# Full-size transposes in a routed mixture of experts: padded gathered rows, a padded threshold, comparisons counted in pairs and a new order

## The chip, the cores and the metric

One core of one Trainium2 chip runs the whole program in one launch. The metric is the device time of an execution in microseconds (us); a kernel's time is the median of several executions. A profiled execution is a separate one and has its own time.

## What is computed

The program chains three stages: masked attention, a two-layer network with a squared ReLU, and a mixture of 8 experts with a greedy assignment of tokens. The change touches the third, whose reference is

```python
def _moe2_ref(x, w_gate, w1, w2):
    N, D = x.shape                      # 1536, 512
    E = w_gate.shape[1]                 # 8
    cap = N // E                        # 192
    flat = (x @ w_gate).flatten()
    order = np.argsort(-flat)
    assigned = -np.ones(N, dtype=np.int64)
    counts = np.zeros(E, dtype=np.int64)
    for idx in order:
        tok, e = (int(idx) // E, int(idx) % E)
        if assigned[tok] >= 0 or counts[e] >= cap:
            continue
        assigned[tok] = e
        counts[e] += 1
        if (assigned >= 0).all():
            break
    out = np.zeros((N, D), dtype=np.float32)
    for e in range(E):
        mask = assigned == e
        h = np.maximum(x[mask] @ w1[e], 0.0)      # w1[e] 512x1024
        out[mask] = h @ w2[e]                     # w2[e] 1024x512
    return out
```

Every expert ends with exactly 192 tokens, its cap.

## The kernel before, in words

Attention takes the first 260 us, the two-layer network runs to about 545 us, router and experts to the end. All matrix work goes through the one instruction queue of TensorE (PE). PSUM banks are named psS, psTP, psm, psO; ff and rf are the zones of SBUF that the third stage uses (rf for fp32r data and raw weights), f and r those of the first two.

**The router** finds the assignment in 8 phases. A phase ranks the remaining tokens by their best logit (rank): for each tile of 128 tokens VectorE (DVE, L1357), or ScalarE for some tiles (ACT, L1353 and L1355), makes a 0/1 tile G in bf16 that compares all values with those of the tile, and PE multiplies each G with the tiles' choices Bb (L1364), 12 matmuls for 12 tiles, later 9 and 6 for fewer tokens. There are four G buffers for DVE. The sums tell which expert fills first and at which value. That threshold is a minimum over tokens and partitions (rest): L1404 reduces to 128x8, L1409 transposes it on PE to 8x128, L1412 reduces that to a column xm of 8 rows, L1415 transposes the column, broadcast, back to all partitions, and L1417 goes on from there. The rest of a phase takes the full expert's tokens out and packs their numbers with the slot constants (L1477) into ix (L1487). The slot constants are four casts on GpSimd (POOL, L1088). The counts are bf16 and nearly everything else on PE is fp32. Short bf16 filler matmuls (L1094) are put on PE where the planner sees it idle.

**An expert** p, in the order in which experts fill, has 192 tokens. POOL gathers their rows with two indirect DMAs (L1676), 128 rows into g[0] and 64 rows into g[1], and then copies the expert's number (L1681), on which the loads of weight groups 1 to 3 wait; group 0 is loaded from the first copy. SyncE (SP) reads the number (L1671) and issues the loads of w1 and w2 (L1633, L1634), 512 KB each. xt_pe transposes the gathered rows, two calls of four transposes: 128x128 ones for the first 128 rows (L1694) and 64-row ones for the other 64 (L1696). The 192 columns of each half are evacuated by ACT and DVE (L1708, L1710; from expert 5 on L1701, L1703). The first layer is L1790 (experts 0 to 4, 128x192 outputs) or L1748 and L1749 (experts 5 to 7); its results go through ReLU by L1801 on ACT and L1804 on DVE (later L1757, L1760, L1762, L1765) and the second layer is L1861 to L1868, where L1868 handles 64 of the 192 rows. Weights are split into two parts by L1644 (ACT) and L1646 (DVE, for some of expert 6's on POOL). Results are scaled by L1924 to L1928 and scattered by L1915 (POOL).

**What sets the order.** Nothing is ordered by hand. A list planner (class Sched) gets every step as an operation with an engine, an assumed duration, the operations that it needs, a priority and the buffers that it takes and releases. Each engine takes the ready operation with the best priority; going between bf16 and fp32 work on PE has an assumed extra. The instructions are issued in the planned order, and semaphores follow the dependencies. The priorities are the numbers in three tables: EP (L1008, the early part of the router), RP (L1016, its phases) and FP (L1594, the experts).

A step in the planner's terms, here the count of one tile:

```python
c.append(S.add("PE", .0252 * n, lambda k=k: g_pe(k), [a, st["z"], st["Bb"], c[-1] if c else None], prio=RP["gp"], w=CW, half=1))
```

Of the kernel before, what the change touches and what calls it, by code (L numbers as in the profile page):

```python
# [7 lines left out]
F32 = mybir.dt.float32  # L8
R = mybir.dt.float32r
BF = mybir.dt.bfloat16  # L10
F16 = mybir.dt.float16
# [993 lines left out]
    return [ld[n] for n in range(12)], st, [i for f in range(16) for i in Wd[f]], []  # L1005


EP = {"fr": 1921.5, "lr": -1861, "row": -1588, "col": 174, "cp": 2028, "ca": -84.5, "gp": 1193}  # L1008
CP = (5, 2, 4, 2, 1, 0)
CA = (3, 0, 2, 4, 1, 4)  # L1010
EP_POOL = (3, 6, 8)
# [1 line left out]
HUGE = 1.5e38  # L1013
SQUEEZE = (2, 4)
ND = 4
RP = {"fr": 2216, "se": 1209, "oh": -1168.5, "G": 471, "A": -1078.5, "lr": -1735.5, "pf": -2953, "id": -1707, "gp": -701, "sq": 1077, "G1": -1034, "A1": 839, "ei": -1539.5, "up": -1158.5}  # L1016
ACT_TILES = {12: (10, 11), 9: (8,), 6: ()}
KEEP = 60
CW = .05
# [17 lines left out]
class Router:  # L1037
# [18 lines left out]

    def pools(self, tc, ctx):
        c = ctx.enter_context(tc.tile_pool(name="rcs2", bufs=1))
        for nm, shape, dt in (("alive", [12], F32), ("pad", [1], F32), ("zero", [128], BF), ("ones", [128], BF), ("tri", [128], BF), ("tok", [12], F16),
                              ("L1", [9, 8], F32), ("alive1", [9], F32), ("tok1", [9], F16),  # L1060
                              ("L2", [6, 8], F32), ("alive2", [6], F32), ("tok2", [6], F16)):
# [8 lines left out]
    def smalls(self, S, deps):  # L1070
        k, P = self.k, self.nc.gpsimd
        alive, tok = self.alive, self.tok

        def small():
            P.memset(alive, 1.0)
            P.memset(self.alive1, 1.0)
            P.memset(self.alive2, 1.0)
            P.memset(self.zero, 0.0)
            P.memset(self.ones, 1.0)
            P.tensor_copy(self.tri, k[:, 0:128])  # L1080
            P.tensor_copy(tok, k[:, 272:284])
        return [S.add("POOL", 1.5, small, deps, prio=MB + 60)]
# [260 lines left out]
    def rank(self, st, ph):  # L1343
        nc, S, n = self.nc, self.S, self.n
        V = nc.vector
        T = self.T
        W = 128 * n

        def g_dve(k, part):
            s = T["mx"][:, k:k + 1]  # L1350
            G, Gt = (self.mem(x, [W], BF) for x in (T["G", k], self.GT))
            if part == 1:
                nc.scalar.activation(Gt, T["lr"], AF.Relu, scale=-1.0, bias=s)  # L1353
            elif part == 2:
                nc.scalar.activation(G[:, 0:W], Gt, AF.Sign)  # L1355
            else:
                V.tensor_scalar(G[:, 0:W], T["lr"], s, None, op0=OP.is_lt)  # L1357

        def g_pe(k):
            Rv = T["R"][:, 0:8 * n].rearrange("p (i e) -> p i e", e=8)  # L1360
            G = self.mem(T["G", k], [W], BF)
            done.append(k)
            for i in range(n):
                nc.tensor.matmul(Rv[:, i], G[:, 128 * i:128 * i + 128], T["Bb"][:, k], start=False, stop=(len(done) == n and i == n - 1))  # L1364

        act = ACT_TILES.get(n, ())
        done = []
        gp = {"a": [], "d": []}
        gt = None
        for k in [*act, *(k for k in range(n) if k not in act)]:  # L1370
            w = "a" if k in act else "d"
            c = gp[w]
            m = 2 if k in act else 4
            war = c[-m] if len(c) >= m else None
            T["G", k] = (self.GA if m == 2 else self.G)[len(c) % m]
# [5 lines left out]
            c.append(S.add("PE", .0252 * n, lambda k=k: g_pe(k), [a, st["z"], st["Bb"], c[-1] if c else None], prio=RP["gp"], w=CW, half=1))  # L1381
        st["rank"] = st["lr"] = [c[-1] for c in gp.values() if c]
        st["unit"] = "B"


    def rest(self, st, ph):
# [8 lines left out]
        def dve(dur, fn, deps, p=RP["se"], rel=None):  # L1395
            return S.add("DVE", dur, fn, deps, prio=p, rel=rel)
# [194 lines left out]
        st["L"], st["alive"], st["tok"] = a, None, e1  # L1591


FP = {"s1": -1097, "ga": -1236, "xp": 853.5, "xe": -539.5, "m1": 866, "re": -510.5, "m2": 30.5, "ye": -493.5, "yt": 339, "yo": -2034, "sc": -2189.5, "sp": -163, "mr": 866}  # L1594
AP = 5
HP, XP = 0, 5
RSLACK, ESLACK = 0, 0.2
# [12 lines left out]
def experts(tc, nc, S, ps, mem, ident, router, x2d, w1, w2, out, L, cst, slot):  # L1610
# [6 lines left out]
    def unit(key, r):  # L1617
        return S.unit(T[key], r)
# [44 lines left out]
    def xr(p):  # L1663
        return "xT" if p < XP else "xR"

    def before(p):
        RT, ids, ei = next(phases)
        RTs[p] = RT

        def vl(i):  # L1670
            T["ev", p, i] = nc.sync.value_load(RT["ei"][0:1, i:i + 1], min_val=0, max_val=7)  # L1671

        def gather():
            g = xg(p)
            for h, n in ((0, 128), (1, 64)):
                nc.gpsimd.indirect_dma_start(out=g[h][0:n], out_offset=None, in_=x2d, in_offset=bass.IndirectOffsetOnAxis(ap=RT["ix"][0:n, h:h + 1], axis=0))  # L1676

        T["v", p, 0] = S.add("SP", .1, lambda: vl(0), [ei], prio=p)
        weights(p, 0, 0)
        T["ga", p] = ga = S.add("POOL", 2.7 if p else 3.8, gather, [ids], prio=FP["ga"], acq="xg")  # L1680
        e2 = S.add("POOL", .1, lambda: nc.gpsimd.tensor_copy(RT["ei"][:, 1:2], RT["ei"][:, 0:1]), [ga, ei], prio=-1)  # L1681
        gd = S.add("DMA", 1.2, None, [ga], prio=-1, lat=1.8)
        T["v", p, 1] = S.add("SP", .1, lambda: vl(1), [e2], prio=p)

        def tv(q):
            return ps(unit(("xt", p, q), "B"))[:, 0:384].rearrange("p (c s) -> p c s", c=2)

        def xt_pe(q):
            g = xg(p)
            for h in (0, 1) if q == 0 else (1, 0):  # L1690
                for c in range(2):
                    cc = 2 * q + c
                    if h == 0:
                        nc.tensor.transpose(tv(q)[:, c, 0:128], g[0][:, 128 * cc:128 * cc + 128], ident)  # L1694
                    else:
                        nc.tensor.transpose(tv(q)[:, c, 128:192], g[1][0:64, 128 * cc:128 * cc + 128], ident[0:64, 0:64])  # L1696

        def xt_hl(q, j):
            o = xT(p)[:, 2 * q:2 * q + 2]
            if j == 0:  # L1700
                nc.scalar.activation(o[:, :, 0], tv(q), AF.Copy)  # L1701
            else:
                nc.vector.tensor_tensor(o[:, :, 1], tv(q), o[:, :, 0].bitcast(F32), op=OP.subtract)  # L1703

        def xt_ev(q):
            o = xT(p)[:, 2 * q:2 * q + 2]
            if q == 0:
                nc.scalar.activation(o, tv(q), AF.Copy)  # L1708
            else:
                nc.vector.tensor_copy(o, tv(q))  # L1710

        xd, a = [], None
        for q in range(2):
            T["xt", p, q] = a = S.add("PE", .44, lambda q=q: xt_pe(q), [gd, a], prio=FP["xp"], acq=("B",) if q else ("B", xr(p)), rel=[("xg", ga)] if q else (), w=.6)
# [327 lines left out]
```

## Time and profile before

| | |
|---|---|
| median of 3 executions | 769.29 us (769.22 to 770.6) |
| the profiled execution | 773.7 us |
| its span | 771.9 us |
| mean granted clock of TensorE | 0.986 |
| PE busy | 751.4 us, 97% of the span |
| DVE busy | 562.4 us, 73% |
| ACT busy | 451.1 us, 58% |
| POOL busy | 399.7 us, 52% |
| DMA | 94.33 MB, mean 122 GB/s |

Busy shares are means over three stages with different limits. The stage of router and experts is read from the timeline and the waits of its own stretch. In the rows below a start is when the engine began an instruction or a run of equal ones, the second column is how long the row lasted, and PE rows overlap, since PE takes the next matmul while the last one runs out: what an instruction costs in a row of others is the distance between starts. "64*128" in a PE row is a tile of 64 rows of the array.

### The profile page before, as it was taken

How to read it: one execution, taken by the hardware profiler on the slowest of the kernel's cores; microseconds unless marked ns; L12 is line 12 of the kernel's file. 1: busy time of each engine (PE TensorE's matmuls, PEld its weight loads, DVE VectorE, ACT ScalarE, POOL GpSimd, SP SyncE). 2: the span in 40 equal slices, each digit the busy share in tenths (PEclk: the TensorE clock that was granted, in tenths of full speed). 3: DMA queues.
4: the chain of work that ended last, by engine and by line, in shares of the span. 5: the costliest groups of instructions: out<-in, count | busy, mean ns of one | idle time of the engine just before them, and what ended most of it. 6: DMA issues, size and time to landing. Idle time of an engine off the chain costs nothing.

```text
span 771.9 us, 13993 instructions
## 1 busy us (share of the span) xinstructions
PE 751.4 (97%) x4950; PEld 655.8 (85%) x4950; DVE 562.4 (73%) x1171; ACT 451.1 (58%) x900; POOL 399.7 (52%) x401
## 2 busy tenths in 40 slices
PE   8989999999999999999999999999999999999996
PEld 6768889879897899999999999999768888888885
DVE  5869989989899967831771484134897888888883
ACT  6969999989998855542343334224443543345772
POOL 2667778768788975752463365215921112222621
PEclk9999999999999999999999999999889999999998
DMA  6976586476640141410131110020136466478901
GB/s 157 244 165 144 115 175 150 102 159 143 157 103 2 56 164 64 153 57 1 55 113 51 53 58 1 0 82 28 56 114 235 154 229 212 152 259 312 349 26 37
DMA packets 87973, 94.33 MB, mean 122 GB/s; under 512 B 41920, under 2 KB 66880, under 8 KB 87904
## 3 DMA queue, kind: packets, MB, share of 16 engines
q1 hardware_dynamic: 85856, 87.16, 40.0%
q0 software_dynamic: 2048, 6.29, 2.6%
q8 instruction: 39, 0.64, 0.3%
q14 instruction: 30, 0.25, 0.1%
HBM read 63.55 MB, written 6.29 MB: 90 GB/s over the span
## 4 chain that ended last, share of the span: by engine, by line
PE 74%; DVE 8%; issue 5%; POOL 4%; ACT 4%; DMA 3%; SPq 1%; ACTq 0%; POOLq 0%; DVEq 0%
PE psS L829 11%; PE psTP L802 9%; PE psm L802 9%; PE psS L1790 6%; PE psS L578 4%; DVE p L626 3%; PE psTP L829 3%; PE psO L829 3%; PE psTP L614 2%; DVE f L594 2%; PE psS L1865 2%; PE psS L1861 2%; POOL f L606 2%; PE psS L1868 2%; PE psS L1862 2%
## 5 line engine op out<-in xcount | busy, mean ns | idle before, releaser
L606 POOL TENSOR_TENSOR f<-f 128x768 f32<-128x768 f32 x96 | 140.8, 1469 | 30.2 <-PE psTP L614 10.2
L815 POOL TENSOR_TENSOR r<-f,r 128x384 fp32r<-128x384 f32 x64 | 86.6, 1359 | 90.5 <-ACT r L813 77.9
L594 DVE TENSOR_REDUCE f<-psS 128x1 f32<-128x768 f32 x96 | 90.9, 948 | 7.6 <-PE psS L578 7.4
L829 PE MATMUL psS<-r 128*128 128x512 f32 x384 | 95.9, 395 | 0.0
L578 PE MATMUL psS<-r 128*128 128x384 f32 x384 | 88.4, 352 | 1.4 <-DMA r<-r 0.8
L597 ACT ACTIVATE f<-psS,f 128x768 f32<-128x768 f32 x96 | 87.1, 907 | 4.2 <-DVE f L603 1.4
L811 DVE TENSOR_TENSOR f<-f,psTP 128x384 f32<-128x384 f32 x32 | 17.7, 554 | 88.7 <-ACT f L809 88.4
L829 PEld LDWEIGHTS psS<-r 128*128 128x128 f32 x384 | 70.8, 188 | 13.1
L802 PE MATMUL psTP<-r 128*128 128x384 f32 x384 | 73.4, 338 | 0.7 <-POOL r L792 0.7
L802 PE MATMUL psm<-r 128*128 128x384 f32 x384 | 71.8, 334 | 0.0
L802 PEld LDWEIGHTS psTP<-r 128*128 128x128 f32 x384 | 67.9, 188 | 3.1 <-POOL r L792 1.0
L578 PEld LDWEIGHTS psS<-r 128*128 128x128 f32 x384 | 65.9, 190 | 5.3 <-ACT f L597 3.3
L802 PEld LDWEIGHTS psm<-r 128*128 128x128 f32 x384 | 67.1, 188 | 0.1
L1915 POOL DMA_INDIRECT out_dram<-ff,ix x16 | 17.9, 1116 | 83.8 <-DVE ff L1926 27.0
L1790 PE MATMUL psS<-ff,rf 128*128 128x192 f32 x320 | 61.0, 332 | 0.0
L626 DVE TENSOR_TENSOR p<-psTP,p 128x384 fp32r<-128x384 f32 x102 | 54.8, 546 | 4.9 <-ACT p L622 4.5
L813 ACT ACTIVATE r<-f 128x384 fp32r<-128x384 f32 x64 | 33.5, 523 | 39.3 <-DVE f L811 39.3
L1676 POOL DMA_INDIRECT ff<-x2d,ix x16 | 19.4, 1210 | 69.9 <-DVE ck L1549 17.7
L792 POOL TENSOR_TENSOR r<-f,r 128x1024 fp32r<-128x1024 f32 x16 | 40.4, 2526 | 28.4 <-ACT r L790 28.1
L1644 ACT ACTIVATE ff<-rf 128x1024 fp32r<-128x1024 f32 x32 | 33.8, 1055 | 34.8 <-PE psS L1863 25.2
L622 ACT ACTIVATE p<-psTP 128x384 fp32r<-128x384 f32 x102 | 49.3, 499 | 7.6 <-PE psTP L614 6.4
L1790 PEld LDWEIGHTS psS<-ff,rf 128*128 128x128 f32 x320 | 52.0, 190 | 1.9 <-DVE ff L1710 0.3
(400 smaller groups left out, 1860.9 us busy)
## 6 DMA issues: line engine op xcount, KB each, us to landing
rf<-in_moe_w_dram SPq DMA_DIRECT2D x64, 512.0 KB, 4.0
r<-r SPq DMA_DIRECT2D x90, 192.0 KB, 4.0
f<-in_moe_w_in_dram SPq DMA_DIRECT2D x16, 512.0 KB, 3.7
f<-in_moe_w_out_dram SPq DMA_DIRECT2D x16, 512.0 KB
r<-r SPq DMA_DIRECT2D x15, 384.0 KB
f<-in_q_dram SPq DMA_DIRECT2D x8, 384.0 KB
f<-in_k_dram SPq DMA_DIRECT2D x8, 384.0 KB
f<-in_v_dram SPq DMA_DIRECT2D x8, 384.0 KB, 3.8
```

The source lines that it names most:

```text
L578: nc.tensor.matmul(sbank(u)[:, hf, 0:384], T["q", (pr, h)][:, n, 128 * i:128 * i + 128], T["k", (pr, h)][:, n, 384 * hf:384 * hf + 384], s ...
L594: nc.vector.tensor_reduce(col(0, u), sbank(u)[:, :, 0:384], axis=AX.XY, op=OP.max, negate=True)
L597: nc.scalar.activation(P(u).rearrange("p (a b) -> p a b", a=2), sbank(u)[:, :, 0:384], AF.Exp, bias=col(0, u), accum_out=col(1, u))
L606: nc.gpsimd.tensor_tensor(Pn(u), P(u), col(3, u).to_broadcast([128, 768]), op=OP.mult)
L622: nc.scalar.activation(th, tp(u, g), AF.Copy)
L626: nc.vector.tensor_tensor(tl, tp(u, g), th.bitcast(F32), op=OP.subtract)
L792: nc.gpsimd.tensor_tensor(lo, F, hi.bitcast(F32), op=OP.subtract)
L802: nc.tensor.matmul(hbank(s, hf), w[:, c], y[:, x, sl], start=(c == 0 and i == 0), stop=(c == 3 and i == 2))
L815: nc.gpsimd.tensor_tensor(hl[:, sl], r, hh[:, sl].bitcast(F32), op=OP.subtract)
L829: nc.tensor.matmul(abank(i), a[:, t], w, start=(f == RUNS[r][1][0] and j == 0), stop=(f == RUNS[r][1][-1] and j == 2))
L1644: nc.scalar.activation(h(p, g, 0), w, AF.Copy)
L1790: nc.tensor.matmul(abank(n)[:, j], raw(p, g)[:, 0, 256 * c + 128 * j:256 * c + 128 * j + 128], xT(p)[:, c], start=(c == 0), stop=(c == 3))
```

## The change

1. The gathered rows are always transposed as 128x128: g[1] is read over all 128 rows. Its rows 64 to 127 are set to zero once by a new POOL operation (two memsets of 64x512, one for each of the two buffers), and the gather writes only rows 0 to 63. The evacuations read the first 192 of 256 columns. Both calls now take g[0] first.
2. The column xm is a lasting 128x1 tile, zeroed once; the transpose that spreads it (L1415) is 128x128 in place of 8 rows to 8 columns.
3. On DVE's tiles the counts are issued for two tiles together, as one operation of the planner, save the last two tiles (LONE). ACT's tiles are counted alone as before.
4. The three tables have other numbers, and so the planner finds another order for router and experts. Attention and the two-layer network keep theirs.

```diff
-EP = {"fr": 1921.5, "lr": -1861, ...
+EP = {"fr": 1831, "lr": -1863.5, ...
+LONE = 2
-RP = {"fr": 2216, "se": 1209, ...
+RP = {"fr": 2209, "se": 1249, ...
...
+            P.memset(self.xm, 0.0)
...
-        def g_pe(k):
+        def g_pe(ks):
             Rv = T["R"][:, 0:8 * n].rearrange("p (i e) -> p i e", e=8)
-            G = self.mem(T["G", k], [W], BF)
-            done.append(k)
-            for i in range(n):
-                nc.tensor.matmul(Rv[:, i], G[:, 128 * i:128 * i + 128], T["Bb"][:, k], start=False, stop=(len(done) == n and i == n - 1))
+            for k in ks:
+                G = self.mem(T["G", k], [W], BF)
+                done.append(k)
+                for i in range(n):
+                    nc.tensor.matmul(Rv[:, i], G[:, 128 * i:128 * i + 128], T["Bb"][:, k], start=False, stop=(len(done) == n and i == n - 1))
...
+            pend.append((k, a))
+            if len(pend) == 2 or ds.index(k) >= len(ds) - LONE:
+                c += [S.add("PE", .0252 * n * len(pend), lambda ks=[x[0] for x in pend]: g_pe(ks), [*(x[1] for x in pend), st["z"], st["Bb"], c[-1] if c else None], prio=RP["gp"], w=CW, half=1)] * len(pend)
+                pend.clear()
...
-        a = dve(.2, lambda: V.tensor_reduce(t("xm", [1])[0:8], T["xp"][0:8, 0:128], axis=AX.X, op=OP.min), [a])
+        a = dve(.2, lambda: V.tensor_reduce(self.xm[0:8], T["xp"][0:8, 0:128], axis=AX.X, op=OP.min), [a])
         def y_pe():
-            nc.tensor.transpose(T["xp"][:, 128:136], T["xm"][0:8].to_broadcast([8, 128]), self.ident[0:8, 0:8])
+            nc.tensor.transpose(T["xp"][:, 128:256], self.xm.to_broadcast([128, 128]), self.ident)
...
-FP = {"s1": -1097, "ga": -1236, ...
+FP = {"s1": -1161.5, "ga": -1309.5, ...
...
-            for h in (0, 1) if q == 0 else (1, 0):
+            for h in range(2):
                 for c in range(2):
                     cc = 2 * q + c
-                    if h == 0:
-                        nc.tensor.transpose(tv(q)[:, c, 0:128], g[0][:, 128 * cc:128 * cc + 128], ident)
-                    else:
-                        nc.tensor.transpose(tv(q)[:, c, 128:192], g[1][0:64, 128 * cc:128 * cc + 128], ident[0:64, 0:64])
+                    nc.tensor.transpose(tv(q)[:, c, 128 * h:128 * h + 128], g[h][:, 128 * cc:128 * cc + 128], ident)
...
+    def pad():
+        for u in UNITS_F["xg"]:
+            nc.gpsimd.memset(mem(u + 2, [512])[64:128], 0.0)
+    T["pad"] = S.add("POOL", 1.0, pad, L, prio=-3)
```

**PE, the transposes of expert 1's gathered rows** (L1694 and L1696 are L1705 after the change; behind them L1326, transposes of the router's next phase, is L1328). Before:

```order
L1865 MATMUL psS_5659<-ff_5223,rf_5214 128x512
L1868 MATMUL psS_5659<-ff_5224,rf_5214 64x512
L1694 MATMUL psTP_60<-ident,ff_5227 128x128 x2
L1696 MATMUL psTP_60<-ident,ff_5227 128x64 x2
L1696 MATMUL psTP_61<-ident,ff_5227 128x64 x2
L1694 MATMUL psTP_61<-ident,ff_5227 128x128 x2
L1326 MATMUL psO<-ident,mx 128x128 x4
```

After:

```order
L1874 MATMUL psS_5664<-ff_5225,rf_5216 128x512
L1877 MATMUL psS_5664<-ff_5226,rf_5216 64x512
L1705 MATMUL psTP_60<-ident,ff_5229 128x128 x4
L1705 MATMUL psTP_61<-ident,ff_5229 128x128 x4
L1328 MATMUL psO<-ident,mx 128x128 x4
```

The place is the same; the four 64-column outputs became 128-column ones.

**PE, counts and second layer in the phase of 9 tiles**, some 3 us further on. A count block is 9 pairs of LDWEIGHTS and MATMUL (L1364 before, L1367 after). Before, one block stood between the two halves of a group of the second layer (L1865, L1868):

```order
L1364 MATMUL psTP_61<-Bb,ff_5237 128x8
L1865 MATMUL psS_5659<-ff_5220,rf_5212 128x512
L1868 MATMUL psS_5659<-ff_5220,rf_5212 64x512
L1364 LDWEIGHTS ff_5238
L1364 MATMUL psTP_61<-Bb,ff_5238 128x8
```

After, the group stands together and the counts of two tiles follow it:

```order
L1799 MATMUL psS_5256<-ff_5231,rf_5207 128x192 x3
L1874 MATMUL psS_5664<-ff_5222,rf_5214 128x512
L1877 MATMUL psS_5664<-ff_5222,rf_5214 64x512 x2
L1874 MATMUL psS_5664<-ff_5222,rf_5214 128x512
L1367 LDWEIGHTS ff_5239
```

From the first expert on, the queue went over to counts and back 38 times before and does so 33 times now; it holds 29 fillers before and 32 after.

**POOL, near the end** (L1676 gathers, L1681 copies an expert's number, L1914 and L1915 scatter; after the change L1688, L1693, L1923 and L1924). Before, from expert 6's gather on:

```order
L1676 DMA ff_5226<-x2d,ix 64x512
L1681 COPY ei<-ei 128x1
L1914 MEMSET pad 128x1
L1915 DMA out_dram<-ff_5234,ix 1536x512
L1914 MEMSET pad 128x1
L1915 DMA out_dram<-ff_5233,ix 1536x512
L1676 DMA ff_5227<-x2d,ix 128x512
L1676 DMA ff_5227<-x2d,ix 64x512
L1681 COPY ei<-ei 128x1
```

After:

```order
L1688 DMA ff_5228<-x2d,ix 64x512
L1688 DMA ff_5229<-x2d,ix 128x512
L1688 DMA ff_5229<-x2d,ix 64x512
L1923 MEMSET pad 128x1
L1924 DMA out_dram<-ff_5236,ix 1536x512
L1693 COPY ei<-ei 128x1 x2
L1923 MEMSET pad 128x1
L1924 DMA out_dram<-ff_5235,ix 1536x512
```

Expert 7's gather moved ahead of a scatter and of expert 6's copy, and the two copies stand together. On SP the second reading of expert 7's number, which needs expert 7's copy, moved ahead of the loads of expert 6's groups 1 to 3.

## Rows read from the trace of the kernel before

**Rows 1.** Busy time by stretch, 584.5 to 600 us (PE first).

```profile
584.50:600.00 15.50, 15.50 (x131) 13.53 (x130) 12.99 (x47) 4.87 (x8) 2.14 (x4) 1.00 0.59 192
```

**Rows 2.** Waits of PE from 584 to 766 us: total, times, longest.

```profile
PE psS L1865 <- DVE rf L1804: 0.5, 1, 0.5
```

**Rows 3.** Timeline around 584 us: start, duration, engine, line, operands, [idle before].

```profile
583.69 0.62 DVE L1804 SCALAR_TENSOR_TENSOR rf<-psS,rf 128x128 fp32r<-128x128 f32 x2
...
584.03 0.51 PE L1865 MATMUL psS<-ff,rf 128*128 128x512 f32 x1 [0.48 <-DVE rf L1804]
```

**Rows 4.** Timeline of PE, expert 1's transposes and those behind them.

```profile
598.16 0.38 PE L1694 MATMUL psTP<-ident,ff 128*128 128x128 f32 x2
...
599.14 0.60 PE L1326 MATMUL psO<-ident,mx 128*128 128x128 f32 x4
599.58 0.60 PE L1326 MATMUL psm<-ident,mx 128*128 128x128 f32 x4
```

**Rows 5.** Timeline of PE, expert 6's transposes, first row, and the matmul behind.

```profile
722.45 0.38 PE L1694 MATMUL psO<-ident,ff 128*128 128x128 f32 x2
...
723.34 0.48 PE L1861 MATMUL psS<-ff,rf 128*128 128x512 f32 x1
```

**Rows 6.** Timeline of PE, expert 2's transposes with a count block between.

```profile
629.53 0.41 PE L1694 MATMUL psTP<-ident,ff 128*128 128x128 f32 x2
...
630.14 0.38 PE L1364 MATMUL psTP<-Bb,ff 128*128 128x8 bf16 x9
630.45 0.33 PE L1696 MATMUL psO<-ident,ff 64*128 64x64 f32 x2
...
630.91 0.48 PE L1865 MATMUL psS<-ff,rf 128*128 128x512 f32 x1
```

**Rows 7.** Timeline of PE, expert 4's transposes with L1415 between.

```profile
677.15 0.38 PE L1694 MATMUL psTP<-ident,ff 128*128 128x128 f32 x2
...
677.73 0.22 PE L1415 MATMUL psm<-ident,xm 8*128 8x8 f32 x1
...
678.41 0.49 PE L1790 MATMUL psS<-ff,rf 128*128 128x192 f32 x2
```

**Rows 8.** Timeline of PE, L1415 among the first layer's matmuls, to 580.6 us.

```profile
579.13 0.82 PE L1790 MATMUL psS<-ff,rf 128*128 128x192 f32 x4
579.88 0.22 PE L1415 MATMUL psm<-ident,xm 8*128 8x8 f32 x1
580.03 0.76 PE L1790 MATMUL psS<-ff,rf 128*128 128x192 f32 x3
```

**Rows 9.** Timeline of PE, first layer between two count blocks.

```profile
602.48 0.57 PE L1790 MATMUL psS<-ff,rf 128*128 128x192 f32 x2
602.89 0.37 PE L1364 MATMUL psTP<-Bb,ff 128*128 128x8 bf16 x9
```

**Rows 10.** Timeline of POOL and DVE at the start of the stage.

```profile
553.31 4.41 POOL L1088 CAST ff<-rck 128x384 f16<-128x384 f32 x4
...
552.79 0.17 DVE L1197 TENSOR_TENSOR Bb<-w,m 128x8 bf16<-128x8 f32 x1
...
557.28 0.46 DVE L1197 TENSOR_TENSOR Bb<-w,m 128x8 bf16<-128x8 f32 x1
...
565.58 0.96 DVE L1477 TENSOR_TENSOR ff<-ff,pk 128x1536 f16<-128x1536 f16 x1
```

**Rows 11.** DMA issues of 700 to 732 us (to landing), and timeline of POOL and ACT.

```profile
rf<-in_moe_w_dram SPq DMA_DIRECT2D x16, 512.0 KB, 8.4
...
710.05 0.54 POOL L1681 COPY ei<-ei 128x1 int32<-128x1 int32 x1
...
714.74 1.67 POOL L1676 DMA_INDIRECT ff<-x2d,ix  x1 [0.32 <-issue]
...
722.40 1.05 ACT L1644 ACTIVATE rf<-rf 128x1024 fp32r<-128x1024 f32 x1
```

**Rows 12.** Busy time by stretch, 570 to 573.5 us; the last three columns are granted clock, DMA share, GB/s.

```profile
570.00:573.50 3.50, 3.50 (x48) 1.83 (x45) 3.50 (x5) 3.20 (x3) 3.19 (x3) 0.51 0.26 75
```

More of the change, by code (lines that the diff above doesn't have):

```diff
@@ L1005, in mlp @@
     return [ld[n] for n in range(12)], st, [i for f in range(16) for i in Wd[f]], []
-EP = {"fr": 1921.5, "lr": -1861, "row": -1588, "col": 174, "cp": 2028, "ca": -84.5, "gp": 1193}
+EP = {"fr": 1831, "lr": -1863.5, "row": -1595, "col": 240.5, "cp": 2055.5, "ca": 20, "gp": 1115}
+LONE = 2
 CP = (5, 2, 4, 2, 1, 0)
@@ L1015 @@
 ND = 4
-RP = {"fr": 2216, "se": 1209, "oh": -1168.5, "G": 471, "A": -1078.5, "lr": -1735.5, "pf": -2953, "id": -1707, "gp": -701, "sq": 1077, "G1": -1034, "A1": 839, "ei": -1539.5, "up": -1158.5}
+RP = {"fr": 2209, "se": 1249, "oh": -1149, "G": 534, "A": -1001.5, "lr": -1816.5, "pf": -2980, "id": -1672, "gp": -626.5, "sq": 1082, "G1": -962, "A1": 813, "ei": -1561.5, "up": -1135.5}
 ACT_TILES = {12: (10, 11), 9: (8,), 6: ()}
@@ L1058, in pools @@
         c = ctx.enter_context(tc.tile_pool(name="rcs2", bufs=1))
-        for nm, shape, dt in (("alive", [12], F32), ("pad", [1], F32), ("zero", [128], BF), ("ones", [128], BF), ("tri", [128], BF), ("tok", [12], F16),
+        for nm, shape, dt in (("alive", [12], F32), ("pad", [1], F32), ("xm", [1], F32), ("zero", [128], BF), ("ones", [128], BF), ("tri", [128], BF), ("tok", [12], F16),
                               ("L1", [9, 8], F32), ("alive1", [9], F32), ("tok1", [9], F16),
@@ L1369, in rank @@
         gt = None
+        pend = []
+        ds = [k for k in range(n) if k not in act]
         for k in [*act, *(k for k in range(n) if k not in act)]:
@@ L1373, in rank @@
             m = 2 if k in act else 4
-            war = c[-m] if len(c) >= m else None
-            T["G", k] = (self.GA if m == 2 else self.G)[len(c) % m]
+            j = len(c) + (len(pend) if w == "d" else 0)
+            war = c[j - m] if j >= m else None
+            T["G", k] = (self.GA if m == 2 else self.G)[j % m]
             if k in act:
@@ L1380, in rank @@
                 a = S.add("DVE", .13 + .00052 * W, lambda k=k: g_dve(k, 0), [*st["lrd"], war], prio=RP["G1" if ph == 1 else "G"])
-            c.append(S.add("PE", .0252 * n, lambda k=k: g_pe(k), [a, st["z"], st["Bb"], c[-1] if c else None], prio=RP["gp"], w=CW, half=1))
+            if w == "a":
+                c.append(S.add("PE", .0252 * n, lambda k=k: g_pe([k]), [a, st["z"], st["Bb"], c[-1] if c else None], prio=RP["gp"], w=CW, half=1))
+                continue
+            pend.append((k, a))
+            if len(pend) == 2 or ds.index(k) >= len(ds) - LONE:
+                c += [S.add("PE", .0252 * n * len(pend), lambda ks=[x[0] for x in pend]: g_pe(ks), [*(x[1] for x in pend), st["z"], st["Bb"], c[-1] if c else None], prio=RP["gp"], w=CW, half=1)] * len(pend)
+                pend.clear()
         st["rank"] = st["lr"] = [c[-1] for c in gp.values() if c]
@@ L1591, in squeeze @@
         st["L"], st["alive"], st["tok"] = a, None, e1
-FP = {"s1": -1097, "ga": -1236, "xp": 853.5, "xe": -539.5, "m1": 866, "re": -510.5, "m2": 30.5, "ye": -493.5, "yt": 339, "yo": -2034, "sc": -2189.5, "sp": -163, "mr": 866}
+FP = {"s1": -1161.5, "ga": -1309.5, "xp": 816.5, "xe": -655, "m1": 866, "re": -351.5, "m2": 30.5, "ye": -493.5, "yt": 339, "yo": -2032, "sc": -2225, "sp": -162.5, "mr": 866}
 AP = 5
@@ L1685, in tv @@
         def tv(q):
-            return ps(unit(("xt", p, q), "B"))[:, 0:384].rearrange("p (c s) -> p c s", c=2)
+            return ps(unit(("xt", p, q), "B")).rearrange("p (c s) -> p c s", c=2)
         def xt_pe(q):
             g = xg(p)
-            for h in (0, 1) if q == 0 else (1, 0):
+            for h in range(2):
                 for c in range(2):
                     cc = 2 * q + c
-                    if h == 0:
-                        nc.tensor.transpose(tv(q)[:, c, 0:128], g[0][:, 128 * cc:128 * cc + 128], ident)
-                    else:
-                        nc.tensor.transpose(tv(q)[:, c, 128:192], g[1][0:64, 128 * cc:128 * cc + 128], ident[0:64, 0:64])
+                    nc.tensor.transpose(tv(q)[:, c, 128 * h:128 * h + 128], g[h][:, 128 * cc:128 * cc + 128], ident)
         def xt_hl(q, j):
@@ L1700, in xt_hl @@
             if j == 0:
-                nc.scalar.activation(o[:, :, 0], tv(q), AF.Copy)
+                nc.scalar.activation(o[:, :, 0], tv(q)[:, :, 0:192], AF.Copy)
             else:
-                nc.vector.tensor_tensor(o[:, :, 1], tv(q), o[:, :, 0].bitcast(F32), op=OP.subtract)
+                nc.vector.tensor_tensor(o[:, :, 1], tv(q)[:, :, 0:192], o[:, :, 0].bitcast(F32), op=OP.subtract)
         def xt_ev(q):
@@ L1707, in xt_ev @@
             if q == 0:
-                nc.scalar.activation(o, tv(q), AF.Copy)
+                nc.scalar.activation(o, tv(q)[:, :, 0:192], AF.Copy)
             else:
-                nc.vector.tensor_copy(o, tv(q))
+                nc.vector.tensor_copy(o, tv(q)[:, :, 0:192])
         xd, a = [], None
         for q in range(2):
-            T["xt", p, q] = a = S.add("PE", .44, lambda q=q: xt_pe(q), [gd, a], prio=FP["xp"], acq=("B",) if q else ("B", xr(p)), rel=[("xg", ga)] if q else (), w=.6)
+            T["xt", p, q] = a = S.add("PE", .44, lambda q=q: xt_pe(q), [gd, a, T["pad"]], prio=FP["xp"], acq=("B",) if q else ("B", xr(p)), rel=[("xg", ga)] if q else (), w=.6)
             if p >= XP:
```

## The prediction, written before the change was run

> **What bounds the kernel now.** I read first the busy time by stretch, then the list of waits on TensorE (PE), then its timeline, row by row. In 584.5 to 600 us PE is busy 15.50 of 15.50 us [rows 1], and in the whole stretch from 584 to 766 us the list of its waits has a single entry: 0.5 us, once, for line L1804 [rows 2]. So from 584 us the end of the program is the sum of what PE does, one instruction behind the other, and whatever shortens a PE instruction there comes off the time, as long as no engine that feeds PE turns out late instead. Before 584 us it is otherwise. The one wait stands at 584.03, where L1865, the second layer of expert 0, waits for the last half of L1804 (583.69) [rows 3]. That chain starts with the slots of expert 0 and goes over its gather, its weights and their splitting, none of which the PE work of 575 to 584 us holds up. What PE saves there only makes this wait longer, and what it saves earlier in the stage is one L1415. I therefore count PE savings only after 584.03.
>
> **The transposes of the gathered rows (L1694, L1696).** The columns to read are the start of a row and the start of the next: the durations of single rows overlap. Expert 1's group runs from 598.16 to 599.14, 0.98 us for four 128-row transposes and four 64-row ones [rows 4]. What a full 128x128 transpose costs in a row of such is in the same group: four of L1326 take from 599.14 to 599.58, 0.11 each. Eight full ones would be 0.88. So a group that stands alone gains 0.98 - 0.88 = 0.10, though it issues wider transposes: a 64-row one is no dearer by itself, but going into and out of the 64-row form is (next paragraph). Four such groups lie after 584 (experts 1, 3, 6, 7): 0.40. Expert 6's group is 0.89 by its starts [rows 5], because what stands behind it is a 512-column matmul whose next start is late by the rest; I use it for groups followed by such a matmul.
>
> In expert 2's group a block of counts lies between the two halves: 629.53 to 630.91 is 1.38, the block 0.31 of it (630.14 to 630.45) [rows 6]; 1.38 - 0.31 - 0.89 = 0.18 is the second way into and out of the 64-row form. The change keeps a block there, with only full transposes around it: 0.10 + 0.18 = 0.28. In expert 4's group L1415 lies between the halves: 677.15 to 678.41 is 1.26 [rows 7], 0.28 over the 0.98; a full transpose in its place leaves 0.11, so it gains 0.17 + 0.10 = 0.27. Expert 5's group has L1415 at its head; I take the same 0.27. Together 0.40 + 0.28 + 0.27 + 0.27 = 1.22 us. Expert 0's group stands before 584.03 and counts nothing.
>
> One thing speaks against this: a padded transpose could show the load of its weights, which is hidden now. The rows have four full ones at 0.11 each with nothing between them [rows 4], so I take none as shown; the last rival prices it. The Trainium skill (TensorE: Matmul & The Clock Gate, Part 3) states that a weight load overlaps a running matmul only when the row groups differ, by which the sum would have such a load for every padded transpose. The four of L1326, all on the same rows, disagree.
>
> **L1415 as a full transpose.** It is an 8-row transpose now. Among L1790 matmuls, which take (0.82 - 0.49)/2 = 0.165 us each (four against two) [rows 7, 8], its surroundings are: 579.13 to 579.88 is 0.75 for four, 0.09 too long; L1415 to the next start 0.15; the three behind it 0.76 where 0.49 + 0.165 = 0.65 is due, 0.11 too long [rows 8]. That is 0.35 against 0.11 for a full one: 0.24 gained. Three of the seven stand so after 584; two are in the groups above and two stand before 584: 0.72 us. The zeros in rows 8 to 127 are set once, before the stage, and L1412 writes the same 8 rows as before.
>
> **Counting in pairs.** One block of counts is bf16 among fp32 work. Two L1790 between two blocks take 602.48 to 602.89, 0.41 against 0.33 due [rows 9]: 0.08 for going over and coming back. By the order on PE there are 38 such trips from the experts' start before and 33 after: 5 x 0.08 = 0.40 us. The counts themselves stay. What waits longer is the first tile of a pair's buffer; the G buffers are four, so VectorE (DVE) can be two tiles ahead, and no PE work is queued for want of it that was not before.
>
> **The new work.** The two memsets of 64 x 512 and the new place of the four slot casts are on POOL. Before, the casts run 553.31 to 557.72 [rows 10], ahead of the stage's start. The memsets write in the zone that L1247, L1254 and L1258 fill and L1268's counts read, so they, and the casts behind them, now wait until PE's last counts, which follow L1197 (done at 557.74). Behind the casts in POOL's queue is expert 0's gather; the slots are first read by L1477 at 565.58, and even casts as slow as before, 4.41 us for the four, with two memsets taken at the same 1.1 each, end by about 564.4, those last counts added. The price lies in DVE. L1197 on 128x8 took 0.17 without a cast beside it and 0.46 beside one, ending as the cast ends [rows 10]: 0.29 us, on the chain that leads to 584.03. The change takes this one away and puts the casts beside the next two-input operations of the same chain. The ends: a gain of 0.29 if the casts then hit none, and a loss of 1.16 if each of the four hits one. I take a loss of 0.15, the middle of one to two hits less the one removed, as L1197 is the nearest row. The Trainium skill (SBUF — State Buffer, Who interferes with whom) lets a DVE operation with two SBUF inputs wait for a GpSimd operation that reads SBUF, and not for one that only writes; by it the memsets would cost DVE nothing, and only the casts count, as I have it.
>
> The late move on POOL puts expert 7's gather in front of a scatter and of expert 6's copy of its number (L1681), and on SP the second reading of expert 7's number, which needs the copy next to expert 6's, ahead of expert 6's weight groups 1 to 3. I cost it at nothing: the copy is at 710.05, a load of that stretch takes 8.4 us to land, so an estimate for these weights is 718.5, and the split of the first of these groups starts on ScalarE (ACT) at 722.40: 3.95 us of cover [rows 11]. Three POOL DMAs ahead of it at 1.67 each would take 5.0, at the shortest rows less; I expect the cover to be just enough, and below that is the slower rival.
>
> **The sum.** 1.22 + 0.72 + 0.40 - 0.15 = 2.19 us off the profiled 773.7 (span 771.9), thus 771.5. The profiled execution is 4.4 above the median of the three runs; I take the same off the median: 769.29 - 2.19 = **767.1 us**.
>
> **The rivals.**
> *The casts hit the chain.* For it: the casts do stretch a DVE operation [rows 10], and the router's operations from 558 on stand one behind the other. Against it: most of them read PSUM or one SBUF operand. With 1.16 in place of 0.15: 769.29 - 2.34 + 1.16 = 768.1, no measurable change (I call within 0.2%, 1.54 us, the same; that is what a measurement here can tell). Chance 0.12.
> *The form change isn't the cause.* The late starts around 64-row and 8-row transposes may belong to something that stays (the turn to a transpose and back). Then L1415 gains nothing, and the 28 padded transposes cost 0.11 in place of (0.98 - 4 x 0.11 - 0.18)/4 = 0.09, 0.56 more: 769.29 + 0.56 - 0.40 + 0.15 = 769.6, the same. Against it: L1326 behind a transpose shows no late start [rows 4]. Chance 0.07.
> *The clock falls at 577.* In the order of the rank phase before it the fillers (L1094) stand in fewer, longer runs with longer blocks of counts between them. In 570 to 573.5, amid such counts and fillers, the granted clock is 0.51, at the lower of its two levels (1.2 of 2.4 GHz) [rows 12]. Should this come at 577 to 581, the 20 L1790 there cost 0.165 more each, 3.3; the wait at 584.03 hides about 0.5, and 769.29 - 2.19 + 2.8 = 769.9, the same. Chance 0.07.
> *Slower: expert 6's weights come late.* The copy moves back by up to 5.0 us and the loads then meet the next gather and a fuller queue. ACT executes in order, so a split that waits holds expert 7's evacuations and the first layer's behind it, and PE waits for those. To come out slower it must eat 2.19 + 1.54 = 3.7 us beyond the cover, that is, land 7.7 us later than now: the 5.0 and 2.7 us of queueing. It decides from a landing after about 726; at 726.7 the time is 769.29 - 2.19 + 4.2 = 771.3. Chance 0.08.
> *Slower: the weight loads show.* Were each of the 28 padded transposes held up by a load as long as itself, 0.11, it would be 28 x 0.11 = 3.1 more in place of 1.22 less: 769.29 + 3.1 - 0.72 - 0.40 + 0.15 = 771.4. L1326 speaks against it [rows 4]. Chance 0.02.
>
> **How the numbers follow.** The forecast has 0.64. Faster 0.64; same 0.12 + 0.07 + 0.07 = 0.26; slower 0.10. Low end: the sum with the 0.29 gained on POOL, the wait of 0.48 at 584.03 gone [rows 3] and the swallowed 0.52 of PE before it (expert 0's group 0.28, L1415 0.24) counted: 769.29 - 2.34 - 0.29 - 0.48 - 0.52 = 765.7. High end: 769.7, which takes in the casts and the form change and leaves out the clock and both slower cases, 0.17. The range of the likeliest case alone is 765.7 to 767.7.
>
> **What would show it.** Right: the groups of eight transposes take 0.88 us by starts, L1415 0.11 among L1790, the list of PE's waits after 584 stays at one entry, and the stretch from that wait to the last matmul is 2.3 us shorter. The casts stand at 558 to 561, L1197 at 0.17, the wait at 584.03 moves by under 0.5 either way. Wrong: PE waits for L1765 or L1646 after 718, expert 6's split begins with a wait for its DMA, the clock row shows a low level after 577, or the end of the wait at 584 moves by over 1 us.

## The result, and the profile after

The changed kernel is slower: a median of 773.89 us (771.26 to 776.1, 14 executions) against 769.73 us (767.63 to 772.06, 14 executions), a ratio of 1.0051 with a 95% interval of 1.0036 to 1.0066. By the ratio that is 3.9 us more (the medians lie 4.2 apart), where 2.2 less were forecast, and outside the range.

The loss isn't where the change was made. The rows of the first instruction of the two-layer network (L802) say when attention is done; its weight load has first and last start behind the durations. Of the kernel before:

```profile
L802 PEld LDWEIGHTS psm<-r x384: 187/188/189, 260.3 to 530.6; 128*128 128x128 f32 x192
```

Of the changed kernel:

```profile
L802 PEld LDWEIGHTS psm<-r x384: 186/188/188, 265.7 to 535.9; 128*128 128x128 f32 x192
```

Attention ends 5.4 us later, and no instruction of it was touched or reordered. The two profiled executions divide so, at L802 and at the first L1865 of expert 0 (L1874 after), the matmul behind the wait of [rows 3]:

| | before | after | |
|---|---|---|---|
| attention, to L802 | 260.3 | 265.7 | +5.4 |
| L802 to expert 0's L1865 | 323.7 | 322.0 | -1.7 |
| from there to the end of the span | 187.9 | 185.7 | -2.2 |
| span | 771.9 | 773.4 | +1.5 |

The profiled execution of the kernel before (773.7) lies above all its 14 timed ones, so the medians differ by more than these two spans. Attention's length varies from one execution to the next: over the profiles of all runs below, L802 begins at 255.4 to 260.3 us in the eleven whose zones (next paragraphs) stand where they did or 256 bytes on. Two profiles alone therefore don't show that the change costs attention its time; the runs with moved zones do.

What differs in attention is its DMA. The DMA view of the first 250 us gives for each kernel packets, MB and the time that these took as a share of 16 engines, and below it the time from issue to landing. Before:

```profile
DMA packets 48474, 35.03 MB, mean 140 GB/s; under 512 B 39712, under 2 KB 40608, under 8 KB 48448
...
q1 hardware_dynamic: 48448, 34.72, 62.2%
...
r<-r SPq DMA_DIRECT2D x90, 192.0 KB, 4.0
```

After:

```profile
q1 hardware_dynamic: 48448, 34.72, 68.3%
...
r<-r SPq DMA_DIRECT2D x90, 192.0 KB, 4.3
...
f<-in_q_dram SPq DMA_DIRECT2D x8, 384.0 KB, 6.2
f<-in_k_dram SPq DMA_DIRECT2D x8, 384.0 KB, 6.7
```

(For q and k the trace before has no landing; the first run below gives 5.2 and 5.9 us.) PE waits longer for these DMAs (total, times, longest, to 545 us), before and after:

```profile
PE psS L578 <- DMA r<-r: 0.8, 1, 0.8
```

```profile
PE psS L578 <- DMA r<-r: 2.9, 1, 2.9
```

The engines' own instructions are not slower: in the first 250 us a 128x768 reduction of L594 takes 948 ns before and 946 after, one of POOL's L606 1469 and 1468.

The same 48448 packets and 34.72 MB take a tenth more DMA time (68.3 / 62.2 = 1.10). The instructions are the same; their addresses are not. The lasting column xm is a new tile that takes 32 bytes per partition, and a small pool lost its two buffers for the old one, 64 bytes. The three big zones, opened behind these pools, start 32 bytes lower. Worked out from the two built programs (SBUF bytes, and the start modulo 256):

```
zone   before        after
r0      26368 (0)     26336 (224)
f0     145152 (0)    145120 (224)
p0     190720 (0)    190688 (224)
```

Behind attention the third stage did what the change set out to do. Expert 1's transposes [rows 4] now stand as one row, and take 601.79 to 602.67, 0.88 us:

```profile
601.79 1.04 PE L1705 MATMUL psTP<-ident,ff 128*128 128x128 f32 x8
602.67 0.60 PE L1328 MATMUL psO<-ident,mx 128*128 128x128 f32 x4
```

L1415 (now L1427) among the first layer's matmuls [rows 8] costs 584.22 to 584.34, 0.12, and the four before it take 0.65 where they took 0.75:

```profile
583.57 0.82 PE L1799 MATMUL psS<-ff,rf 128*128 128x192 f32 x4
584.22 0.28 PE L1427 MATMUL psm<-ident,xm 128*128 128x128 f32 x1
584.34 3.42 PE L1799 MATMUL psS<-ff,rf 128*128 128x192 f32 x20
```

The waits of PE from 545 to 770 us (total, times, longest) hold no new one on L1646 or L1765 (L1658 and L1774 now), and the 0.5 us on L1804 [rows 2] is gone; a wait of 0.8 on the router's L1445 is new. The first row was 1.7 before:

```profile
PE psS L1266 <- DVE Bb L1197: 1.7, 1, 1.7
```

```profile
PE psS L1268 <- DVE Bb L1199: 1.0, 1, 1.0
PE psm L1157 <- DVE mm L1445: 0.8, 1, 0.8
PE psTP L1367 <- ACT ff L1357: 0.4, 1, 0.4
PE psS L1799 <- DVE ff L1719: 0.3, 1, 0.3
```

### The profile page after: what moved, and what is told of

It reads as the page before. It is cut to its first block, busy times and chain, and to the rows that moved or that the text cites. A ratio compares the mean times of both kernels' runs of the same rounds, so it can differ in the third digit from the quotient of the medians.

```text
span 773.4 us, 14015 instructions
## 1 busy us (share of the span) xinstructions
PE 746.2 (96%) x4953; PEld 655.7 (85%) x4953; DVE 560.1 (72%) x1171; ACT 450.9 (58%) x900; POOL 398.2 (51%) x404
## 4 chain that ended last, share of the span: by engine, by line
PE 76%; DVE 6%; issue 4%; DMA 4%; ACT 4%; SPq 3%; POOL 2%; ACTq 0%; POOLq 0%; DVEq 0%
PE psS L829 11%; PE psTP L802 9%; PE psm L802 9%; PE psS L1799 6%; PE psS L578 5%; SPq L259 3%; PE psTP L614 3%; DMA f<-in_v_dram 3%; PE psTP L829 3%; PE psO L829 3%; PE psS L1874 2%; PE psS L1870 2%; PE psS L1877 2%; PE psS L1871 2%; PE psS L1872 2%
## 5 line engine op out<-in xcount | busy, mean ns | idle before, releaser
L606 POOL TENSOR_TENSOR f<-f 128x768 f32<-128x768 f32 x96 | 140.7, 1468 | 31.5 <-PE psTP L614 11.6
L594 DVE TENSOR_REDUCE f<-psS 128x1 f32<-128x768 f32 x96 | 90.8, 946 | 12.5 <-PE psS L578 12.3
L802 PE MATMUL psTP<-r 128*128 128x384 f32 x384 | 73.4, 338 | 0.7 <-POOL r L792 0.7
L802 PE MATMUL psm<-r 128*128 128x384 f32 x384 | 71.7, 334 | 0.0
L802 PEld LDWEIGHTS psTP<-r 128*128 128x128 f32 x384 | 67.9, 188 | 3.1 <-POOL r L792 1.0
L802 PEld LDWEIGHTS psm<-r 128*128 128x128 f32 x384 | 67.1, 188 | 0.1
L1924 POOL DMA_INDIRECT out_dram<-ff,ix x16 | 17.8, 1112 | 79.5 <-DVE ff L1935 41.4
L809 ACT ACTIVATE f<-psTP 128x384 f32<-128x384 f32 x32 | 15.7, 489 | 64.6 <-PE psTP L802 63.3
```

Source lines behind the costliest of these rows:

```text
L594: nc.vector.tensor_reduce(col(0, u), sbank(u)[:, :, 0:384], axis=AX.XY, op=OP.max, negate=True)
L606: nc.gpsimd.tensor_tensor(Pn(u), P(u), col(3, u).to_broadcast([128, 768]), op=OP.mult)
L802: nc.tensor.matmul(hbank(s, hf), w[:, c], y[:, x, sl], start=(c == 0 and i == 0), stop=(c == 3 and i == 2))
```

## The experiments

Two theories at first. A: the zones' 32 bytes slow the DMAs of attention, and the third stage gains. B: the order, or chance, costs attention its time and addresses play no part. In each run "the rest" is the span from the first L802 on.

### The zones moved, nothing else

**The changed kernel with its zones back.** One more unused tile, 32 bytes:

```diff
-("tok", [12], F16),
+("tok", [12], F16), ("gap0", [1], F32),
```

> The changed kernel with one unused 128x1 tile more, which moves the three big SBUF zones from 26336 to 26368 bytes, their place in the kernel before (a multiple of 256). Theory A (the changed kernel loses in attention, since its zones start 32 bytes off a multiple of 256 and every SBUF end of a DMA with them): the first layer L802 begins near 260 us as before, not at 265.7, the rest keeps its gain of about 3.9 us, and the time is about 766, some 8 below the changed kernel and 3 to 4 below the one before. Theory B (the loss is one of the order or of the executions themselves, addresses play no part): still about 774.

Measured: 765.72 us against 769.85, ratio 0.9945 (0.9926 to 0.9963). L802 begins at 259.1, and the DMA time is that of the kernel before:

```profile
L802 PEld LDWEIGHTS psm<-r x384: 187/188/188, 259.1 to 529.3; 128*128 128x128 f32 x192
```

```profile
q1 hardware_dynamic: 48448, 34.72, 62.2%
...
f<-in_q_dram SPq DMA_DIRECT2D x8, 384.0 KB, 5.2
f<-in_k_dram SPq DMA_DIRECT2D x8, 384.0 KB, 5.9
```

32 unused bytes are worth 1.0051 / 0.9945 = 1.07%, some 8 us. This version beats both kernels.

**The kernel before, moved by 224 bytes** (seven such tiles, so that its zones stand modulo 256 where the changed kernel's do):

> The kernel before with seven unused 128x1 tiles, which move the zones by 224 bytes, so that they start 224 above a multiple of 256 as in the changed kernel; nothing else differs. Theory A: L802 begins 5 us or more later than at 260, the copies of 192 KB land later than 4.0 us, and the time is about 775 to 778 (769.7 plus 5 to 8). Theory B: the time of the kernel before, 769.7 within 1.5.

Measured: 778.85 us, ratio 1.0111 (1.0094 to 1.0128), the same price from the other side. The rest is 778.2 - 266.6 = 511.6, as in the kernel before (771.9 - 260.3); all of the loss lies ahead of L802:

```profile
L802 PEld LDWEIGHTS psm<-r x384: 186/188/188, 266.6 to 536.8; 128*128 128x128 f32 x192
```

```profile
q1 hardware_dynamic: 48448, 34.72, 67.9%
...
f<-in_q_dram SPq DMA_DIRECT2D x8, 384.0 KB, 6.1
f<-in_k_dram SPq DMA_DIRECT2D x8, 384.0 KB, 7.1
```

**Moved by 256 bytes** (eight tiles), and **by 128** (four):

> The kernel before with eight unused tiles: the zones move by 256 bytes and start at a multiple of 256 again. Theory A: the time of the kernel before, 769.7 within 1.5. A rival to it, that any move of the zones costs: slower as with 224. Theory B: 769.7.

> The kernel before with four unused tiles: the zones start 128 above a multiple of 256. Theory A in its strict form (only multiples of 256 are free): slower by about as much as with 224, 775 or more. A weaker form (a multiple of 64 or 128 is enough): 769.7 as before. Theory B: 769.7.

Measured: with 256, ratio 1.0010 (0.9994 to 1.0026), no change; it isn't the move that costs. There q and k land 5.4 and 5.9 us behind their issue, for the 6.1 and 7.1 above. With 128, 1.0052 (1.0033 to 1.0071), about half the price of 224. Theory B falls, and so do the weaker form of A, by which 128 would do, and the strict one, by which it would cost as much as 224.

q, k and v come in pieces of 64 fp32 values, 256 bytes, and most packets here are under 512 bytes. The Trainium skill (DMA: Bandwidth & Descriptors, How a descriptor splits into AXI transactions) says that a descriptor is cut into transactions of 256 bytes, and that one which doesn't start at a multiple of 256 begins at the multiple below, where the bytes fetched ahead of the start still cost beats of 32 bytes. It tells this of reads, and here the moved end of the loads is the one written. If writes are cut in the same way, an estimate from that page is 8 beats for a piece at 0, 12 at 128 and 15 at 224, so 128 would pay 4/7 of the price of 224. The runs agree with that in the order and about in the size: the DMA time is 65.5% with 128, 3.3 points up, and 5.7 up with 224; in the kernel's time it is 0.52 of 1.11%. Transactions and beats are in no trace here.

**Which zone.** The load zone f0 off by 224 (and p0 above it), then the operand zone r0 alone:

```diff
-mem.zone("r0", 0, (116,))
+mem.zone("r0", 0, (116.21875,))
```

> The kernel before with the zone of the first two stages' loads (f0) and the one above it 224 bytes off a multiple of 256, while the zone of fp32r operands (r0), within which the 192 KB copies run, stays. Theory F (the loads from HBM into f0 pay): L802 begins 5 us or more later than in the kernel before, time 775 or more. Theory R (the copies inside r0 pay, they have both ends there): 769.7 within 1.5.

```diff
+seven tiles as above
-mem.zone("r0", 0, (116,))
+mem.zone("r0", 0, (116.03125,))
```

> The reverse: r0 224 bytes off, f0 and the zone above it on multiples of 256. Theory R: 775 or more and the copies of 192 KB land later than 4.1 us. Theory F: 769.7 within 1.5. If both pay, each alone is 772 to 775.

Measured: f0 alone 1.0085 (1.0058 to 1.0112), r0 alone 1.0023 (1.0009 to 1.0038). The two prices add up to 1.08%, for 1.11% of both. So the zone of the loads from HBM pays three quarters, more than "each alone 772 to 775" had it (776.86), and r0, within which the copies run, the rest (772.27), by an interval that is clear of 1 by little. With f0 off, q lands after 6.3 us while the copies stay at 4.1:

```profile
q1 hardware_dynamic: 48448, 34.72, 65.8%
...
r<-r SPq DMA_DIRECT2D x90, 192.0 KB, 4.1
...
f<-in_q_dram SPq DMA_DIRECT2D x8, 384.0 KB, 6.3
```

With r0 off, q lands nearly as with aligned zones, and the DMA time rises all the same:

```profile
q1 hardware_dynamic: 48448, 34.72, 64.9%
...
f<-in_q_dram SPq DMA_DIRECT2D x8, 384.0 KB, 5.5
```

The DMA time of r0's run rises by 2.7 points and that of f0's by 3.6, so r0 costs much less time for the DMA work it adds.

### The parts of the change, one at a time

All with the zones at their old place, each from one profile. Of the time before expert 0's L1865 and of that behind it, the second is steady: 187.8 to 188.3 in nine of the ten profiles with PE's old order (189.1 in one with new waits), 185.7 and 185.8 in the two with the new one. The first is less so: 322.8 to 324.6 in ten profiles that have the casts and the gather as before, 321.7 to 322.3 in the five that have the memsets ahead of the casts. A single profile's rest is therefore good to about half a microsecond to one.

**The memsets and padded transposes**, and **the memsets alone**:

```diff
+    T["pad"] = S.add("POOL", 1.0, pad, L, prio=-3)
```

> The kernel before with the padded transposes and their two memsets, nothing else; zones where they were. Measured by the rest, from the first L802 to the end of the span: 511.3 to 511.6 us in four kernels with the old third stage, 507.7 and 508.1 in two with the new one. The prediction's terms: 1.22 less for the transposes and 0.15 more for the casts, a rest of 510.4. Rival (the casts' move gains on the chain of the stage's start, as the 0.7 us between 554 and 558 in the changed kernel suggests): 509.5.

> The kernel before with the two memsets alone, which hold the four slot casts back until PE's last counts; the 64-row transposes stay. The prediction: 0.15 more, a rest of 511.6. Rival (moving the casts off L1190, L1247 and L1197 gains): 0.7 less, 510.8, with the first filler run after the last counts 0.7 us earlier behind L802 than in the kernel before.

Measured: the memsets alone give a rest of 509.9, all of it ahead of expert 0's L1865 (322.0 for 323.7; behind it 187.9), although PE, DVE and ACT keep their order to the instruction. With the transposes 509.1; behind L1865 187.1, that is 0.8 less.

**The threshold alone** and **the pairs alone**:

> The kernel before with L1415 as a full transpose of the lasting column (one unused tile more, so that the zones stay). The prediction: 5 of 7 count after 584, two of them among 64-row transposes, 0.72 to 1.06 less, a rest of 510.4 to 510.8. Rival (PE's savings are taken back by waits): 511.5.

> The kernel before with the counts in pairs alone, under the old tables. The prediction: 0.08 us for each trip between counts and fp32 work that goes, 0.40 at most, a rest of 511.1. Rival (the pairs let the rank phase before 577 end earlier or later, through other fillers and another clock): the first L1790 off by 0.5 or more behind L802, either way.

Measured: behind L1865 187.1 and 187.4, so 0.8 and 0.5 less than 187.9; rests 510.5 and 510.2. With a spread of 0.5 among unchanged kernels, the 0.5 of the pairs is the least sure of the three.

**Why the memsets gain.** Two places. First the casts, which had run beside L1190, L1247 and L1197. Before, the four took 4.41 us and L1197 0.46 [rows 10]; in the changed kernel, behind PE's last counts, 1.86 us, and L1197 (now L1199) 0.16. L1190 and L1247, which stand ahead of L1197 (L1192 and L1249 now), gain too. Before:

```profile
555.38 0.47 DVE L1190 SCALAR_TENSOR_TENSOR w<-L,mx,rck 128x8 f32<-128x8 f32 x1
555.96 1.40 DVE L1247 TENSOR_TENSOR f<-f,mx 128x1024 bf16<-128x1024 f32 x1
```

After:

```profile
563.32 1.01 POOL L1972 MEMSET ff<- 64x512 f32 x2 [4.67 <-PE psS L1270]
564.40 1.86 POOL L1090 CAST ff<-rck 128x384 f16<-128x384 f32 x4
...
560.67 0.22 DVE L1192 SCALAR_TENSOR_TENSOR w<-L,mx,rck 128x8 f32<-128x8 f32 x1
561.00 1.21 DVE L1249 TENSOR_TENSOR f<-f,mx 128x1024 bf16<-128x1024 f32 x1
562.13 0.16 DVE L1199 TENSOR_TENSOR Bb<-w,m 128x8 bf16<-128x8 f32 x1
...
565.96 0.31 DVE L1431 SCALAR_TENSOR_TENSOR sc<-sc,th,rck 128x8 f32<-128x8 f32 x1
```

The three are 0.25, 0.19 and 0.30 shorter, 0.74 together, and that is what PE's wait for L1197 lost (1.7 to 1.0 above). A little goes back where the casts stand now: L1431 (L1419 before) had taken 0.23. Expert 0's index is written 307.4 us behind L802 in the five profiles with the casts behind the memsets, and 307.7 to 308.1 in the other eleven.

Second, expert 0's gather. In the kernel moved by 256 it starts 0.98 us behind the end of its index and takes 1.96:

```profile
565.45 0.15 DVE L1487 CAST ix<-psTP 128x2 int32<-128x2 f32 x1
...
566.58 1.96 POOL L1676 DMA_INDIRECT ff<-x2d,ix  x1 [11.83 <-issue]
```

With the memsets alone 0.31 and 1.69:

```profile
562.80 0.15 DVE L1487 CAST ix<-psTP 128x2 int32<-128x2 f32 x1
...
563.26 1.69 POOL L1676 DMA_INDIRECT ff<-x2d,ix  x1 [7.26 <-DVE ix L1487]
```

To separate them, **the casts ahead of the memsets**, and **two more memsets long before**:

```diff
-    T["pad"] = S.add("POOL", 1.0, pad, L, prio=-3)
+    T["pad"] = S.add("POOL", 1.0, pad, [*L, slot], prio=-3)
```

> The kernel before with the two memsets behind the four casts instead of ahead of them: the casts run beside L1190, L1247 and L1197 again, and only the memsets wait for PE's last counts. Theory C (0.75 us of the gain of the memsets alone comes from taking the casts off that chain): the first filler runs 298.06 us behind L802 again, casts 4.4 us long. The rest of that gain, the first gather's start 0.30 in place of 0.97 us behind its index: if it goes with POOL's shorter idle time or with two more instructions in its stream, it stays, and the rest is about 510.6; if it goes with the casts' place, the rest is 511.4.

> The kernel before with two more memsets of a small constant on POOL long before the stage, the casts where they were. Theory I (the first gather's late start goes with its place in POOL's instruction stream): it starts 0.30 us behind its index, and the rest is about 510.7. Theory C (it goes with the casts' place or POOL's idle time, 11.7 us before and 7.3 in the changed kernel): 0.97 us as before, and a rest of 511.4.

Measured: with the casts first, they take 4.4 us again and the first filler is at 298.0 behind L802 (297.3 with the memsets first): the 0.7 us is the casts'. The gather still starts 0.31 behind its index, rest 510.3. With two memsets early it starts 0.95 behind, rest 511.1: the number of instructions in POOL's stream isn't it. Then **one small memset behind the casts**:

> The kernel before with one small POOL memset (128x1, of the scatter's own spare tile) behind the casts, which waits for PE's last counts as the two large ones did. Theory W (the first gather starts 0.30 us behind its index when POOL has done something in the 8 us before): 0.30, rest about 510.3. Theory Z (it needs the memsets of the gather's own buffers): 0.95 to 0.97 as before, rest about 511.4.

Not decided: the small memset had nothing to wait for and ran at once, so POOL again idled 11.5 us, and the gather came 0.97 us late. Over all sixteen profiles, a gather behind 7 to 9 us of idle time was early and behind 11.5 to 11.9 late; but the early ones are just those behind the memsets of its own buffers, so which of the two does it stays open. The rest was 513.7, neither 510.3 nor 511.4: PE waits of 0.7 for an expert's weights and 1.0 for L1404 are in no other profile of the old order, and L1865 waits 0.9.

**The tables.** The changed code with the old numbers, zones back:

> The changed kernel with the zones back at 26368 bytes and the three tables of the kernel before: padded transposes, padded threshold and pairs, planned with the old numbers. Theory T0 (the tables bring nothing of their own): the time of the changed kernel with its zones back, 765.7, and a rest of 507.8 to 508.1. Theory T1 (the tables carry part of the gain): 767 or more, a rest of 509 or more.

Measured: 768.93 us against 771.5, ratio 0.9966 (0.9946 to 0.9987), which overlaps the 0.9945 of the same code with the new tables; rest 509.9. Behind expert 0's L1865 it takes 188.2 us, no less than the kernel before (187.9), although the padded transposes, the threshold and the pairs gained 0.8, 0.8 and 0.5 there one at a time. Its profile has two waits of PE in that stretch that the new tables' lacks (total, times, longest):

```profile
PE psS L1874 <- DVE rf L1774: 1.1, 1, 1.1
PE psTP L1421 <- DVE X L1416: 0.7, 1, 0.7
```

In these two profiles the new numbers are worth 2.4 us of that stretch (188.2 to 185.8), 1.8 of it by keeping such waits out, and 1.8 of the rest. It is one profile each, and the times alone leave it unproved.

## Why the prediction was wrong, point by point

**The sum left out attention.** It began at 545 us. Of the new column the prediction said that its zeros "are set once, before the stage" and gave that no price. The order shows no difference ahead of the stage; the 32 bytes are not in an order. What failed is the step from "the same instructions in the same order" to "the same time": the new tile and the buffers it replaced moved three zones off a multiple of 256, for about 8 us (1.07 and 1.11%, from both sides). None of the rivals had it; the late weights of expert 6, the slower one, did not come about. Expert 6's copy did move back, to 716.01 us, and the split that needs the weights follows at 724.04 without a wait:

```profile
716.01 1.44 POOL L1693 COPY ei<-ei 128x1 int32<-128x1 int32 x2
```

```profile
724.04 1.06 ACT L1656 ACTIVATE rf<-rf 128x1024 fp32r<-128x1024 f32 x1
```

That the cover held was luck by the prediction's own figures. The first of these loads left SP at 718.66; with the 8.4 us of [rows 11] it would have landed at 727.1, 3 us late. It took 4.1, after two microseconds in which the DMA engines were busy to 0.20 and 0.02.

**Behind 584 us the sum was right, with the new tables.** Forecast 1.22 + 0.72 + 0.40 = 2.34; the stretch from expert 0's L1865 on is 187.9 - 185.7 = 2.2 shorter. By parts: the threshold 0.72, measured 0.8; the pairs 0.40, measured 0.5; the transposes 1.22, measured 0.8 with the old L1415 (each from one profile). Of the 1.22, 0.34 was the two places where L1415 stands in a group, which the transposes alone can't gain; 0.88 is left against 0.8. The sum gave the new tables no term; with the old ones the three parts together brought nothing there (188.2), so that the total came out also rests on the tables, which the sum took for granted. That the form change is the cause, and weight loads don't show, is borne out by the 0.88 us of eight transposes, 0.11 each, while each one's weight load takes 0.14. The rule of the Trainium skill on weight loads (TensorE: Matmul & The Clock Gate, Part 3), by which they would show, doesn't hold for these.

**Ahead of 584 us a term had the wrong sign.** The new place of the casts was taken as a loss of 0.15, between a gain of 0.29 and a loss of 1.16. It gained 0.7 by the first filler, outside these bounds: they counted only L1197, while L1190 and L1247 ran beside the casts too. The hit that was feared is there, on L1431, but smaller than what was won (0.08 here, 0.29 with the memsets alone). Nor did the memsets cost DVE nothing, as the prediction had it: beside them L1423 took 0.46 (as L1411 before 0.16), and the chain behind it starts 0.11 later. Another 0.9 came from the first gather (0.67 earlier, 0.27 shorter), which nothing in the sum had. Both lie on the chain that the wait at 584.03 ended, and together they account for the 1.7; by the spread given above that figure is good to about half a microsecond. A move of over 1 us was one of the prediction's own signs of being wrong. The 1.7 us there and the 2.2 behind it are the 3.9 us that the third stage gains, nearly twice the forecast, and about half of what the zones lost.

**The clock** didn't fall behind 577 us: its granted value in 577 to 584.5 is 1.00 (2.4 GHz) in both profiles.

## What to carry to other kernels

A change that adds, drops or resizes any buffer moves what is allocated behind it: compare the start addresses of the DMA buffers of the two built programs, not only their orders, and keep them on multiples of 256 bytes, the only places that cost nothing here. If two profiles differ in a stage that wasn't touched, split the time by stage first and ask what its DMAs see. A gain in a late stage is proved by that stage's own length, from a marker that both kernels have; here the stretch behind expert 0's L1865 was steady to half a microsecond in nine of ten profiles, while attention's length varied by 5. Parts that gain alone need not add up: check them together under the same order.

## What the runs showed of the hardware that was not expected

- 224 bytes off a multiple of 256 cost the DMA-fed attention stage 1.1% of the whole program, 128 bytes half of that, and 256 nothing. The zone of the loads in 256-byte pieces from HBM paid 0.85%, that of the copies of 192 KB within SBUF 0.23%.
- Four casts on POOL took 4.41 us beside DVE's L1190, L1247 and L1197 and 1.86 us away from them, for the same work.
- An indirect DMA on POOL started 0.30 us behind its index after 7 to 9 us without work on POOL, and 0.95 to 0.98 us after 11.5 us or more; why is open.
